# First attention in one hand-written order of TensorE and VectorE, with the Fourier folds inside it

## The chip, the cores and the metric

The kernel runs on one core of a Trainium2 chip, in float32 throughout. Its metric is the device time of one execution in microseconds. Six executions of the kernel before took 844.06 to 846.88 us, with a median of 845.41 us.

## The reference

Two blocks follow each other. The first is a sparse attention over 4 batches, 8 heads, 768 positions and a head dimension of 64. Each query sees the keys less than 16 positions away, and beside them 24 summaries of the whole sequence: for each block of 32 positions the element-wise maximum of its keys and the mean of its values.

```python
k_sum = k.reshape(B, H, nb, block, D).max(axis=3)      # block = 32
v_sum = v.reshape(B, H, nb, block, D).mean(axis=3)
scores_l = where(abs(pos[:, None] - pos[None, :]) < 16, scale * q @ k.T, -1e9)
scores_s = scale * q @ k_sum.T + log(block)
a = softmax(concatenate([scores_l, scores_s]))
x = a @ concatenate([v, v_sum])                        # heads side by side: (4, 768, 512)
```

The second block mixes x by the real part of a Fourier transform over both the sequence and the model dimension, adds it, normalizes, and runs a dense network with 2048 hidden channels. Its weights come in as 64-bit floats.

```python
u = x + real(fft(fft(x, axis=1), axis=2))
un = (u - mean(u)) / sqrt(var(u) + 1e-6)
out = u + maximum(un @ w_ch1, 0) @ w_ch2
```

## The kernel before

The program goes batch by batch: attention of a batch, its Fourier stage, its hidden layer in two halves of eight column groups, and its output products. The stages of different batches overlap. Attention of batch b+1 is issued beside the hidden layer of batch b, and the Fourier stage of b+1 beside the last output products of b. Only the first attention (batch 0) has nothing beside it. It works on four pairs of heads, in a form called wide: 64 queries against 96 positions of keys and 32 rows for the block summaries, so that one product with 128 rows does both.

For each pair, `load` (L568) fetches keys and queries. `prepare` turns them by products with the identity (`qk`, L672), ScalarE copies them out of PSUM into `kt` and `qt`, and VectorE takes the block maxima `km` (L683). `wide_scores` makes the scores in two halves on TensorE (`sc`, L699 and L703), ScalarE takes the exponentials (`p`, L705), and VectorE multiplies with a mask (`p<-p,wide`). `sum_values` brings the block sums of the values into place (`vs` on TensorE, L714; the copy into `vw` on ScalarE, L715). `wide_values` makes the products with the values (`av`, L723), and VectorE divides into `x` (reciprocal at L728, then a multiplication). The block sums of the values come from `block_sums`: four transfers, and additions on GpSimd (POOL), except for one half batch (batch 1, its second), which VectorE adds.

VectorE's `tensor_tensor` is recorded at L560 for all its uses, and GpSimd's at L563, because both go through a helper; transfers through `fetch` are at L547.

The Fourier stage begins with folds on VectorE: sums and differences of the two halves of the sequence (`fold<-x`), then of the two halves of the model dimension, then of mirrored columns (L560, L1006). For batch 0 four products that go nowhere (`busy`, L961; eight rows of the profile) are issued between the folds. Products with the cosine and sine tables follow (`y`, L1024 and L1028), copies into `big` by ScalarE, products over the model dimension (`mx`, L1048, L1050), statistics on VectorE (`bst`, L1056), and normalized, turned columns `u` for the hidden layer (`hx`, `hy`, `hz`, L1111).

While batch 0 passes these stages, `gen_weights` converts the 64-bit weights (loaded as pieces called `words`) on VectorE and ScalarE (L864 to L871) and stores the results for later batches. It starts once the folds of batch 0 are issued.

What sets the order. TensorE's instructions of the first attention stand in program order (`manual_schedule`); other engines' orders are found by a planner, with the Fourier stage ahead by a given priority. The transfers of SP's queue stay in program order up to the hidden layer of batch 0. At most eight transfers are in flight, since SP waits for the one eight places earlier before it issues the next. Buffers set when a load may start: four for keys and queries, two for `vw`.

Of the kernel before, what the change touches and what calls it, by code (L numbers as in the profile page):

```python
# [9 lines left out]
FP = mybir.dt.float32  # L10
# [6 lines left out]
P = 128  # L17
BLOCK = 32
W = 16
# [468 lines left out]
def _main_program(ctx, tc, q, k, v, moe_w_ch1, moe_w_ch2, out):  # L488
# [35 lines left out]

    wide = bpool.tile([P, NC, 2, S], FP, tag="h", name="wide").rearrange("p j h s -> p (j h s)")
    wide, count = wide[:, 0:QB], wide[:, QB:QB + NQ]
# [41 lines left out]
    def load(b, g):  # L568

        qn, kn = (apool.tile([P, 2, NST // 2, 2 * D], FP, tag="nat", bufs=4, name=f"{n}n_{b}_{g}") for n in "qk")  # L570
        for dst, src in ((kn, k), (qn, q)):
            fetch(out=dst.rearrange("p e j n -> p (e j) n"),
                              in_=src[b, 2 * g:2 * g + 2].rearrange("e (j p s) d -> p (e j) (s d)", p=P, s=2))
        nat[b, g] = qn, kn
# [7 lines left out]
    done_weights, sums = [], {}  # L582

    def block_sums(b, gg, g=None):

        rows, heads = (4 * nb, slice(4 * gg, 4 * gg + 4)) if g is None else (2 * nb, slice(2 * g, 2 * g + 2))
        f = BLOCK // 4
        n = f * D
        if done_weights or g == 1:
            raw = room(f"vb_{b}_{gg}") if done_weights else words[:, 4 * n:8 * n]  # L590
            raw = [raw[0:rows, n * i:n * (i + 1)] for i in range(4)]
        else:

            raw = [bpool.tile([P, NC, P], FP, tag="s", bufs=5, name=f"vb_{b}_{gg}_{g}_{i}").rearrange("p n t -> p (n t)")
                   [0:rows] for i in range(4)]
        for i in range(4):
            fetch(out=raw[i], in_=v[b, heads].rearrange("h (n f) d -> (h n) (f d)", f=BLOCK)
                  [:, n * i:n * (i + 1)])
        vb = spool.tile([rows, D], FP, tag="vbs", bufs=2, name=f"vbs_{b}_{gg}_{g}")

        add = tt if (b, gg) == (1, 1) else gtt
# [3 lines left out]
        if (b, gg) == (1, 1):  # L605
# [6 lines left out]
        for n in (2 * gg, 2 * gg + 1) if g is None else (g,):  # L612
            sums[b, n] = vb, sel[0:rows, 0 if g is not None else n % 2]
# [8 lines left out]
    def load_values(b, g):  # L622
        if g % 2 and following(b, g, 1) and (b, g) not in ((0, 1), (1, 1)):
            block_sums(*divmod((b * NP + g + 1) // 2, NP // 2))
        (load_wide_values if is_wide(b) else load_narrow_values)(b, g)

    def load_wide_values(b, g):

        vw = wide_vw(g)
        for e in range(2):  # L630
            off = v[b, 2 * g + e].offset
            parts = [(W, WK, 0, 1), (0, WK, 1, NQ - 1), (0, WK - W, NQ - 1, NQ)]
            for r0, r1, i0, i1 in parts:
                fetch(out=vw[r0:r1, e, i0:i1, 0:D],
                                  in_=bass.AP(v.tensor, off + (QB * i0 - W + r0) * D,
                                              [[D, r1 - r0], [QB * D, i1 - i0], [1, D]]))
# [21 lines left out]
    def prepare(b, g, between=None):  # L658
        qn, kn = nat[b, g]
        kt, km = kt_bufs[g % 2], km_bufs[g % 2]  # L660
        qt = apool.tile([P, S], FP, tag="qt", name=f"qt_{b}_{g}")
        for src, dst in ((kn, kt[:, W:W + S]), (qn, qt)):
            if src is qn and between:
                between()
            if is_wide(b):
                for j0, j1 in ((0, 2), (2, 3)):
                    n = 2 * P * (j1 - j0)
                    ps = abank([P, n], f"qk_{b}_{g}_{j0}")
# [20 lines left out]
    def wide_scores(b, g):  # L689
# [3 lines left out]
        for half in range(2):  # L693
# [10 lines left out]
            for e in range(2):  # L704
                nc.scalar.activation(out=p[:, e, n0:n1], in_=ps[e], func=AF.Exp, scale=SC)  # L705
                tt(p[:, e, n0:n1], p[:, e, n0:n1], wide[:, None, :].to_broadcast([P, NQ // 2, QB]), ALU.mult)
        return p

    def sum_values(b, g):

        ps = abank([P, 2, D], f"vs_{b}_{g}")
        for e in range(2):
            vb, pick = sums[b, g]
            nc.tensor.matmul(ps[WK:P, e], pick[:, D * e:D * e + 32], vb, start=True, stop=True)  # L714
        nc.scalar.copy(out=wide_vw(g)[WK:P, :, :, 0:D],  # L715
                       in_=ps[WK:P, :, None, :].to_broadcast([P - WK, 2, NQ, D]))

    def wide_values(b, g, p, x):
        vw = wide_vw(g)
        av = [abank([P, NST, D1], f"av_{b}_{g}_{e}") for e in range(2)]  # L720
        for n in range(NQ):
            for e in range(2):
                ins = nc.tensor.matmul(av[e][QB * (n % 2):QB * (n % 2 + 1), n // 2, :], p[:, e, n, :], vw[:, e, n, :],  # L723
                                       start=True, stop=True)
        marks["last av"] = ins.ins
        for e in range(2):
            rc = rec[:, b * NP + g, e]
            marks["av", b, g] = nc.vector.reciprocal(out=rc, in_=av[e][:, :, D]).ins  # L728
# [64 lines left out]

    def gen_attention(b):
        x = bpool.tile([P, NST, DM], FP, tag="x", bufs=2, name=f"x_{b}")
        x_of[b] = x
        for g in range(NP):
            p = (wide_scores if is_wide(b) else scores)(b, g)
            yield
            if not is_wide(b):  # L800
                sum_scores(b, g, p[1])
            elif g:
                sum_values(b, g)
            n1, n2 = following(b, g, 1), following(b, g, 2)
            early = (b, g) == (0, NP - 1)
            if early:
                wide_values(b, g, p, x)
            if n1:
                with tc.issue_after(marks["last av"]) if early else ExitStack():
                    prepare(*n1, (lambda: sum_values(0, 0)) if (b, g) == (0, 0) else None)  # L810

            for n in {(0, 1): (), (0, 2): (2,), (0, 3): (2, 3)}.get((b, g), (3,)):
                n = following(b, g, n)
                if n:
                    load(*n)
            yield
            if not early:
                if is_wide(b):
                    wide_values(b, g, p, x)
                else:  # L820
                    values(b, g, *p, x)
            if (b, g) == (0, 0):
                block_sums(0, 1)
                load_raw(2)
# [515 lines left out]
```

## Time and profile before

| What | Time |
|---|---|
| the profiled execution | 845.48 us |
| its span | 843.3 us |
| TensorE busy, matmul | 811.1 us (96%) |
| VectorE busy | 490.8 us (58%) |
| ScalarE busy | 233.0 us (28%) |
| GpSimd busy | 49.8 us (6%) |
| granted TensorE clock, mean | 0.992 |

The span is the time from the first to the last recorded instruction; the execution's own time has some 2.2 us around it. Busy shares are means over stages with different limits. A row of the timeline gives start, length, engine, line, operation, output and inputs, and in brackets the idle time before it with what ended it. The chain of waits follows the work that ended last back to its start. TensorE's f32 products appear as two matmul rows each.

### The profile page before, as it was taken

What the parts mean: (1) busy time and instruction counts of PE and PEld (TensorE: products, weight loads), DVE (VectorE), ACT (ScalarE), POOL (GpSimd) and SP (SyncE); (2) the same over time, 40 slices, a digit from 0 to 9 for tenths busy, and PEclk for the clock granted to TensorE, in tenths of its full rate; (3) what the DMA queues carried; (4) which work ended last, traced back from release to release, by engine and by line L of the source; (5) the groups of instructions that cost most, each with busy time, mean ns of one, the idle gap of its engine ahead of it and who ended that gap; (6) DMA issues with size and microseconds to landing.
All of it is one profiled execution on the core that took longest, in us unless ns stands there. A gap on an engine that the chain in (4) does not pass through costs nothing.

```text
span 843.3 us, 14730 instructions
## 1 busy us (share of the span) xinstructions
PE 811.1 (96%) x6082; PEld 580.7 (69%) x6082; DVE 490.8 (58%) x1117; ACT 233.0 (28%) x497; POOL 49.8 (6%) x57
## 2 busy tenths in 40 slices
PE   7979898999999999999999999999999999999997
PEld 4747555544568865787667875688657885786586
DVE  2478998988898843542447943443338953532352
ACT  2524856452531113122232103220322012101100
POOL 4420002003000200001000000000000000000000
PEclk9999999999999999999999999999999999999999
DMA  7995698988653265453734236403411326205001
GB/s 170 244 275 95 147 311 200 258 258 234 220 182 131 88 203 200 124 110 141 186 101 106 69 125 225 108 25 74 178 57 64 110 61 251 88 1 218 1 26 54
DMA packets 102347, 120.54 MB, mean 143 GB/s; under 512 B 50720, under 2 KB 83712, under 8 KB 102272
## 3 DMA queue, kind: packets, MB, share of 16 engines
q1 hardware_dynamic: 101584, 119.32, 48.1%
q8 instruction: 50, 0.82, 0.4%
q10 hardware_dynamic: 688, 0.20, 0.1%
q14 instruction: 25, 0.20, 0.1%
HBM read 96.96 MB, written 22.54 MB: 142 GB/s over the span
## 4 chain that ended last, share of the span: by engine, by line
PE 81%; DVE 9%; ACT 5%; DMA 2%; issue 1%; ACTq 0%; SPq 0%; DVEq 0%
PE hx L1111 18%; PE ox L1175 16%; PE hz L1111 9%; PE oz L1175 8%; PE hy L1111 4%; PE oy L1175 4%; PE y L1024 4%; PE o L1152 3%; PE sc L740 2%; DVE x L560 2%; PE mx L972 2%; DVE w L560 2%; ACT qt L682 1%; ACT kt L682 1%; PE unt L1089 1%; PE ss L756 1%
## 5 line engine op out<-in xcount | busy, mean ns | idle before, releaser
L1111 PE MATMUL hx<-u,w 128*128 128x384 f32 x512 | 186.3, 492 | 9.6 <-DVE h L560 4.6
L1111 PEld LDWEIGHTS hx<-u,w 128*128 128x128 f32 x512 | 94.2, 190 | 75.2 <-DVE h L560 8.0
L1111 PE MATMUL hz<-u,w 128*128 128x384 f32 x256 | 93.5, 487 | 0.0
L1175 PE MATMUL ox<-w,s 128*128 128x256 f32 x336 | 80.7, 381 | 0.3
L1175 PE MATMUL oz<-w,s 128*128 128x256 f32 x336 | 80.5, 379 | 0.0
L1175 PE MATMUL ox<-w,h 128*128 128x256 f32 x336 | 78.0, 380 | 0.0
L1111 PEld LDWEIGHTS hz<-u,w 128*128 128x128 f32 x256 | 48.4, 190 | 34.8 <-ACT h L1128 1.1
L560 DVE TENSOR_TENSOR x<-ox,x 128x256 f32<-128x256 f32 x84 | 35.3, 423 | 61.2 <-PE ox L1175 61.0
L1175 PEld LDWEIGHTS ox<-w,h 128*128 128x128 f32 x336 | 63.4, 190 | 9.7
L1175 PEld LDWEIGHTS ox<-w,s 128*128 128x128 f32 x336 | 62.7, 190 | 9.5 <-DVE x L560 1.2
L1175 PEld LDWEIGHTS oz<-w,s 128*128 128x128 f32 x336 | 63.5, 190 | 8.4
L560 DVE TENSOR_TENSOR h<-hx,h 128x384 f32<-128x384 f32 x32 | 17.8, 556 | 66.5 <-PE hx L1111 66.5
L560 DVE TENSOR_TENSOR h<-hy,h 128x384 f32<-128x384 f32 x32 | 17.8, 557 | 62.9 <-PE hy L1111 59.7
L1121 ACT COPY h<-hx 128x384 f32<-128x384 f32 x32 | 15.3, 477 | 116.3 <-PE hx L1111 104.6
L1111 PE MATMUL hy<-u,w 128*128 128x384 f32 x128 | 46.5, 486 | 0.0
L1152 PE MATMUL o<-w,h 128*128 128x512 f32 x96 | 43.6, 610 | 0.9 <-DVE w L560 0.9
L1175 PE MATMUL oy<-w,h 128*128 128x256 f32 x168 | 39.7, 379 | 0.0
L1024 PE MATMUL y<-fs,fold 128*128 128x193 f32 x192 | 37.4, 335 | 0.2 <-PE oz L1175 0.2
L1137 ACT ACTIVATE h<-hx 128x384 f32<-128x384 f32 x32 | 15.7, 490 | 79.4 <-PE hx L1111 79.3
L1024 PEld LDWEIGHTS y<-fs,fold 128*128 128x128 f32 x192 | 31.3, 190 | 8.0 <-issue 6.2
L683 DVE TENSOR_REDUCE km<-kt 128x24 f32<-128x768 f32 x16 | 15.2, 952 | 35.3 <-ACT kt L682 24.5
L1111 PEld LDWEIGHTS hy<-u,w 128*128 128x128 f32 x128 | 24.2, 190 | 16.7
(138 smaller groups left out, 1114.3 us busy)
## 6 DMA issues: line engine op xcount, KB each, us to landing
w<-dw SPq DMA_DIRECT2D x44, 896.0 KB, 5.8
words<-in_moe_w_ch_dram SPq DMA_DIRECT2D x32, 512.0 KB, 6.6
dw<-w SPq DMA_DIRECT2D x12, 896.0 KB, 8.4
vw<-in_v_dram SPq DMA_DIRECT2D x47, 192.0 KB, 5.3
kn<-in_k_dram SPq DMA_DIRECT2D x16, 384.0 KB, 4.7
qn<-in_q_dram SPq DMA_DIRECT2D x16, 384.0 KB, 5.6
out_dram<-x SPq DMA_DIRECT2D x24, 256.0 KB, 2.3
fs<-c_fs SPq DMA_DIRECT2D x8, 579.0 KB, 3.8
```

Of the source, the lines that this page charges most:

```text
L560: nc.vector.tensor_tensor(out=out, in0=in0, in1=in1, op=op)
L682: nc.scalar.copy(out=dst[D * e:D * (e + 1), s:S:2], in_=ps[D * s:D * (s + 1)])
L683: nc.vector.tensor_reduce(out=km[:, 0:nb], in_=kt[:, W:W + S].rearrange("p (n f) -> p n f", f=BLOCK), op=ALU.max, axis=AX.X)
L740: nc.tensor.matmul(ps[h][r:r + 64, i, :], kt[rows, o:o + 64], qt[rows, o:o + BLOCK], start=True, stop=True)
L756: nc.tensor.matmul(ps[r:r + 32, :], km[rows, :], qt[rows, S2 * h:S2 * (h + 1)], start=True, stop=True)
L972: nc.tensor.matmul(out, y[:, g], table, start=True, stop=last, skip_group_check=True)
L1024: nc.tensor.matmul(y, fgs[par][:, st, P * g:P * (g + 1)], fs[par][:, g % 2, st, :], start=(st == 0), stop=(st == HT - 1))
L1111: nc.tensor.matmul(ps, w[:, a, kk, :], u[:, r, kk, :], start=start and kk == 0, stop=stop and kk == 1, skip_group_check=True)
L1121: nc.scalar.copy(out=c11, in_=X)
L1137: nc.scalar.activation(out=c21, in_=X, func=AF.Relu)
L1152: nc.tensor.matmul(ps, h[:, n, hf, P * t:P * (t + 1)], wt[2, b, j][:, 2 * hf:2 * hf + 2, :], start=(n, hf) == (0, 0), stop=(n, hf) == (NC ...
L1175: nc.tensor.matmul(ps, left[a][:, n, :], wt[2, b, j][:, r, :], start=start and n == 0, stop=stop and n == NC - 1, skip_group_check=True)
```

## The change

The first attention gets a function of its own, `first_attention`, whose instructions stand in program order on TensorE and on VectorE. A pair's scores are issued before the products with the values of the pair before it. Each pair's columns of `x` are folded over the sequence as soon as they are there (`fold_sequence`), in a place beside the mask; halves are folded when two pairs are there (`fold_halves`), and the mirrored columns after the last pair (`fold_ends`). The products called `busy` are gone.

The block sums of batch 0 are one transfer and five additions on VectorE for each half batch (`add_blocks`), between the two halves of a pair's scores. The block sums of batches 1 and 2 that ran on GpSimd are VectorE additions too, with a reduction at the end (`add = gtt if done_weights else tt`); those of batch 3 stay on GpSimd. For pairs 0 and 3 the copy of the block sums into `vw` is VectorE's.

The loads stand in another order: keys of pair 1 third, tables (`fs`, `fd`, `near`), two weight pieces and the first keys and queries of batch 1 ahead of the values of pair 3. The values' six transfers have the two large ones first. The first pair of batch 1 is prepared in a step of its own after the first attention. The wide transposes take PSUM from the other pool. For batches 1 to 3 the mean and variance come from two ScalarE passes with accumulators in place of VectorE's statistics instructions.

```diff
+    def add_blocks(gg):
+        raw, vb = to_add[gg]
+        n = BLOCK * D // 2
+        while n > D:
+            tt(raw[:, 0:n], raw[:, 0:n], raw[:, n:2 * n], ADD)
+            n //= 2
+        tt(vb, raw[:, 0:D], raw[:, D:2 * D], ADD)
...
+        if b == 0:
+            raw = words[0:rows, 4 * n * gg:4 * n * (gg + 1)]
+            fetch(out=raw, in_=src)
+            to_add[gg] = raw, vb
+            return
...
-        add = tt if (b, gg) == (1, 1) else gtt
+        add = gtt if done_weights else tt
...
-        if (b, gg) == (1, 1):
+        if not done_weights:
             nc.vector.tensor_reduce(out=vb, in_=raw[0].rearrange("p (f d) -> p d f", d=D), op=ADD, axis=AX.X)
...
-                    ps = abank([P, n], f"qk_{b}_{g}_{j0}")
+                    ps = bank([P, n], f"qk_{b}_{g}_{j0}")
...
+            if half == 0 and between:
+                between()
...
-        nc.scalar.copy(out=wide_vw(g)[WK:P, :, :, 0:D],
-                       in_=ps[WK:P, :, None, :].to_broadcast([P - WK, 2, NQ, D]))
+        (nc.vector.tensor_copy if g in (0, NP - 1) else nc.scalar.copy)(
+            out=wide_vw(g)[WK:P, :, :, 0:D], in_=ps[WK:P, :, None, :].to_broadcast([P - WK, 2, NQ, D]))
...
+    def first_attention():
+        x = x_of[0] = bpool.tile([P, NST, DM], FP, tag="x", bufs=2, name="x_0")
+        fold = bpool.tile([P, 7, 2, S2], FP, tag="u", name="fold_0").rearrange("p a k n -> p (a k n)")
+        wt["fold"] = fold[:, 0:3 * HT * DM].rearrange("p (i t d) -> p i t d", i=3, t=HT)
+        p = {0: wide_scores(0, 0, lambda: add_blocks(0))}
+        prepare(0, 1)
+        sum_values(0, 0)
+        load(0, 3)
+        for g in range(NP - 1):
+            p[g + 1] = wide_scores(0, g + 1, (lambda: add_blocks(1)) if g == 1 else None)
+            wide_values(0, g, p[g], x)
+            load_values(*following(0, g, 2))
+            for par in range(2):
+                fold_sequence(par, g)
+            if g == 0:
+                get_tables(0)
+            if g < NP - 2:
+                prepare(0, g + 2)
+                load(1, g)
+                sum_values(0, g + 1)
+            if g == 0:
+                load_raw(2)
+                fetch(out=near, in_=dr["near"].ap().rearrange("p (h i) c -> p h i c", h=2))
+            if g == NP - 3:
+                sum_values(0, g + 2)
+        fold_halves(0, 0)
+        wide_values(0, NP - 1, p[NP - 1], x)
+        for par in range(2):
+            fold_sequence(par, NP - 1)
+            if par:
+                fold_halves(par, 0)
+            fold_halves(par, 1)
+            fold_ends(0, par, wt["fold"][:, par], wt["fold"][:, 2 - 2 * par])
+
+    def fold_sequence(par, g):
+        x, c = x_of[0], slice(P * g, P * (g + 1))
+        tt(early[par][:, :, c], x[:, 0:HT, c], x[:, HT:NST, c], SUB if par else ADD)
+
+    def fold_halves(par, g):
+        sd, zw = early[par], wt["fold"][:, par]
+        lo, hi = slice(P * g, P * (g + 1)), slice(HD + P * g, HD + P * (g + 1))
+        tt(zw[:, :, lo], sd[:, :, lo], sd[:, :, hi], ADD)
+        tt(zw[:, :, hi], sd[:, :, lo], sd[:, :, hi], SUB)
...
-            keep_busy(b, par, sd)
...
-                bst = spool.tile([P, 6], FP, tag="bst", name=f"bst_{b}_{t}")
-                nc.vector.bn_stats(out=bst, in_=x[:, t, :])
-                nc.vector.bn_aggr(out=stat[:, i], in_=bst)
+                nc.scalar.activation(out=un[:, t, :], in_=x[:, t, :], func=AF.Copy, scale=-1.0 / DM,
+                                     accum_out=minus[:, i:i + 1])
+                nc.scalar.activation(out=un[:, t, :], in_=x[:, t, :], func=AF.Square, bias=minus[:, i:i + 1],
+                                     accum_out=var[:, i:i + 1])
...
     load(0, 0)
+    load(0, 1, 1)
+    block_sums(0, 0)
+    load(0, 1, 0)
...
-    with tc.manual_schedule(engines={mybir.EngineType.PE}):
-        drive((first(attn, 6), 1, 0))
...
-    with tc.manual_schedule(engines={mybir.EngineType.PE}):
-        drive((attn, 1, 600), (first(weights, 18), 3, 0))
-    attn = gen_attention(1)
-    drive((gen_fourier(0), 4, 600), (first(weights, 66), 12, 0), (first(attn, 5), 1, 0))
+    with tc.manual_schedule(engines={mybir.EngineType.PE, mybir.EngineType.DVE}):
+        first_attention()
...
+    block_sums(1, 0)
+    def second_attention():
+        prepare(1, 0)
+        load(1, 2)
+        load_values(1, 1)
+        yield
+        yield from gen_attention(1)
+    attn = second_attention()
+    drive((gen_fourier(0), 4, 600), (first(weights, 66), 12, 0), (first(attn, 6), 1, 0))
```

## The prediction

> **What bounds the kernel now.** I read the page first, then busy time by stretch, then the chain of waits over the first 66 us, then the timeline where a wait stood out.
>
> ```profile
> span 843.3 us, 14730 instructions
> PE 811.1 (96%) x6082; PEld 580.7 (69%) x6082; DVE 490.8 (58%) x1117; ACT 233.0 (28%) x497; POOL 49.8 (6%) x57
> ```
>
> TensorE has 32.2 us of idle time in all. The stretches (length, then busy us of PE, PEld, DVE, ACT, POOL, the granted clock, the DMA share, GB/s) say where:
>
> ```profile
> 0.00:10.00 10.00, 8.33 (x66) 5.55 (x68) 1.96 (x14) 3.10 (x5) 2.67 (x9) 1.00 0.77 167
> 10.00:20.00 10.00, 5.82 (x72) 4.07 (x68) 3.03 (x4) 2.33 (x5) 4.80 (x6) 0.89 0.73 177
> 40.00:50.00 10.00, 8.31 (x162) 6.57 (x163) 6.06 (x11) 5.37 (x10) 5.92 (x7) 1.00 1.08 296
> 50.00:60.00 10.00, 6.86 (x47) 3.92 (x43) 8.34 (x12) 0.52 (x4) 0.14 (x1) 0.83 1.15 278
> 80.00:100.00 20.00, 17.46 (x377) 13.70 (x377) 18.50 (x58) 13.19 (x25) 0.00 (x0) 1.00 0.56 115
> 100.00:120.00 20.00, 18.50 (x239) 11.46 (x237) 19.79 (x42) 12.35 (x24) 0.00 (x0) 1.00 0.87 271
> ```
>
> In the first attention (to 51 us) TensorE is idle 8 us and VectorE mostly free, but the DMA engines are at their limit from 20 us on. From 60 to 200 us VectorE is nearly full (Fourier, then the weights' conversion): there it sets the pace with TensorE. After 240 us TensorE stands still for only a few us. The chain (start, length, what) names the early holes:
>
> ```profile
> 10.17 7.20 DMA kn<-in_k_dram
> 17.50 2.57 PE qk L672 x24
> 47.29 0.50 ACT p L705
> 47.80 1.43 ACT vw L715
> 49.26 0.50 ACT p L705
> ```
>
> Pair 1's keys are asked for at 10.17 and land at 17.37; TensorE had ended pair 0's scores at 13.3. The timeline gives the end of the attention, the folds, and three rows for prices used below:
>
> ```profile
> 45.84 0.43 SPq L547 DMA_DIRECT2D near<-c_near  x1
> 46.71 0.38 SPq L547 DMA_DIRECT2D kn<-in_k_dram  x1
> ...
> 49.29 2.03 PE L723 MATMUL av<-vw,p 128*64 128x65 f32 x48 [1.69 <-ACT vw L715]
> 52.56 1.76 DVE L560 TENSOR_TENSOR fold<-x 128x1536 f32<-128x1536 f32 x1
> 54.37 4.54 PE L961 MATMUL busy<-fold,ident 128*128 128x512 f32 x6 [3.06 <-DVE fold L560]
> 64.78 0.55 DVE L1006 TENSOR_TENSOR fold<-fold 128x381 f32<-128x381 f32 x1
> ```
>
> The last attention product ends at 51.3, VectorE folds until 65.3, and only then does it turn to the weights.
>
> **The change, step by step.**
>
> 1. *Loads at the start.* Pair 1's keys are issued third, at about 2 us, and the block-sum values of a half batch in one transfer (2 transfers where there were 12). The 4.2 us wait for keys goes; so does the slow stretch behind it, where 24 transposes took 2.57 us against 1.53 at 27.9: 1.0 us.
>
> 2. *First attention at TensorE's own pace.* By the rows, a pair is 1.53+1.56 transposes, 0.41 sums, 3.9 scores, 1.65 products: 9.1 us. From 13.3: three times 7.4, plus four times 1.65, gives 42.2. VectorE's order is now fixed by hand, and block sums (1024, 512, 256, 128, 64 elements; from 0.68 for 512 and 0.96 for 768, about 2.8 us) stand between two halves of a pair's exponentials' masking. Behind them wait the masking, and behind that the products; also pairs 0 and 3 copy their sums on VectorE (1536 elements, 1.76 by the fold row). VectorE's load for a pair is then about 8 us against 9.1, so most is covered; if it is not, a pair slips by up to 2.8. I add 1.3: **43.5** is TensorE's bound for the end.
>
> 3. *The transfers, the new bound.* SP's queue is in order, and pair 3's values, which waited for their buffer alone, now stand behind the tables (2 fs, fd, near), batch 1's first keys and queries and two weight pieces. Behind them in the queue wait batch 1's next keys, values and weight pieces, which nobody needs before the folds end. Ahead of and with them: 10 keys/queries of 384 KB, 2 sums of 768, 4 values of 560, 1158+768+384 of tables, 1024 of weights, 200 of constants: 11.2 thousand KB, 11.4 MB. Adding the 2 us stretches of the trace, before had moved 11.4 MB at 50.7 us, with about 3 us lost between 16 and 22 us (46 to 180 GB/s). At 290 GB/s throughout it would be 42. By kinds: values at 150 GB/s (6 to 12 us), 512-byte rows at 270 (12 to 14), wide rows at 380 (48 to 54) make 15.3+14.6+13, plus 2.3 to start: 45.2. I take 46.3 for the landing, near the third figure because this queue has fewer small transfers than before. With 1.65 of products and 0.35 of slow clock the attention ends at **48.3**, not 51.25: **-2.95**. Ends: 43.5 (-7.75); and, if the values land only with what stands ahead of them in the queue, 57, where keys issued at 46.71 land now (10.5 us later): 58.9 (+7.6).
>
> 4. *Folds.* From the last product to the last fold VectorE took 14.1 us (51.25 to 65.33). Now only the last pair's share is left: 1.29 for reciprocals and x, 2 sums, 6 halves, 8 ends at 0.50 each (128x384 pitch: two in 1.02), km 0.9, and 0.8 of latency and waiting for the copied keys: 11.0. **-3.1**. The 13 us of other pieces (two block sums 5.6, two copies 3.5, eight fold pieces 4) lie in the first attention, where VectorE was busy 3 to 6 us in 10.
>
> 5. *Batch 1's first pair between.* Its transposes, scores and block scores are now ahead of the Fourier products on TensorE, so those wait for ScalarE's eight copies (4.2 us) and km: about 6.2 us after the last product, where before it was 6.6. No gain there; but km (0.95) no longer comes after the folds, and the 1.20 us that VectorE waited at 69.4 for ScalarE, full of those copies, goes: **-2.15**. The 8 busy products filled a stall and cost nothing.
>
> 6. *Block sums of batches 1 and 2 on VectorE.* Three sets move from POOL: three adds at 0.68 and a reduction of 1.02, 3.07 each. The first, formerly at 43.6 to 49.7 beside the attention, now stands in the full stretch: **+3.07**. The others replace POOL work in that stretch (columns as above):
>
> ```profile
> 126.18 1.27 POOL L563 TENSOR_TENSOR vb_None<-vb_None,vb_None 96x512 f32<-96x512 f32 x1 [74.66 <-DMA vb_None<-in_v_dram]
> 126.30 1.71 DVE L869 SCALAR_TENSOR_TENSOR words<-words 128x512 int32<-128x512 int32 x1 [1.89 <-ACT words L866]
> 130.28 1.50 DVE L864 TENSOR_SCALAR words<-words 128x512 int32<-128x512 int32 x1
> ```
>
> Those take 0.69 and 0.42 elsewhere. Over 126 to 134 VectorE lost 3.0 us, over 191 to 201 2.8. So 6.14 against 5.8: **+0.3** (ends: 0, and 6.1 if none of the slowing mattered).
>
> 7. *Statistics on ScalarE* in batches 1 to 3: 18 times 0.69+0.17 leaves VectorE, 36 passes of about 0.6 (128x512 copy) join ScalarE, at 2 to 6 us in 20 there. TensorE's idle time in those stages is 0.5, 0.1 and 0.1 us. I take 0; ends -0.8 and +3 (one longer tail per batch, if the products beside it run out). The other pool for transposes, and the moved memsets: 0, as those banks stand free.
>
> Sum: -2.95-3.1-2.15+3.07+0.3 = **-4.8**; against the profiled execution (845.48 for a span of 843.3, 0.07 above the median) **840.7**.
>
> *A rule that speaks against it.* The slow clock after the 4.2 us wait (0.50 at 18 to 20 us) cost 1.5 us over transposes and sums; a 3.1 us wait at 132 cost none (clock 1.00 throughout). The Trainium skill, "TensorE: Matmul & The Clock Gate", section "Why this matters for your kernels", wants no idle gap of over about 3 us between bursts, or the clock falls to half. The change drops the products that kept TensorE busy and leaves two such gaps, before the last products and before the Fourier products. Its section "What's actually happening" has full clock come back after about 3.4 us of work. By these both gaps are followed by 3.4 us at half rate, an estimate from that page of 3.4 us lost, and the sum would be 843.8. By the rows I took 0.35 for the first and nothing for the second, which VectorE's folds cover.
>
> **Rivals.** *Slower: the last values come late.* The one queue delivers pair 3's values after 50.1 us. For: the DMA share is already 1.05 to 1.15 from 30 us on. Against: wide rows ran at 355 to 410 GB/s from 46 to 52. Each us late is a us; break-even is an end of attention at 53.1, and landing at 57 gives 851.3. *TensorE's bound holds*, transfers arrive in time: 43.5, thus 835.9. For: fewer transfers; against: step 3's third figure. *The gain is not carried*: VectorE's relief from POOL is not on the path (+5.8), or the weight pieces' transfers (share 1.13 at 120 to 140) set the stage: 846.5 at worst. *The statistics cost*: 843.7, inside the range.
>
> **How the numbers follow.** Forecast 0.50 (838 to 843.5, all faster); TensorE's bound 0.13; not carried 0.17 (0.02 faster, 0.13 same, 0.02 slower); late values 0.20 (0.02 same, 0.18 slower). About 0.2%, 1.7 us, can be told from no change. So faster 0.65, same 0.15, slower 0.20. Range: 835.5, TensorE's bound, to 847, which leaves out most of the late-values case.
>
> **What would show it.** Right: pair 1's transposes follow scores at about 13.3 without a wait; no row for busy products; attention ends at 46 to 50, the wait before it naming values; last fold near 59; first hidden product 5 us before its present 97.6; no POOL rows at 126 or 191 and no VectorE row of 1.5 us beside them. Wrong: values for pair 3 landing after 50, VectorE's block sums ahead of masking holding TensorE in each pair, or the same first hidden product and a longer weights stage.

## The result and the profile after

| | before | after |
|---|---|---|
| median of the runs | 846.19 us | 842.81 us (840.22 to 848.12) |
| the profiled execution, its span | 845.48, 843.3 us | 843.82, 842.0 us |
| ratio to before | | 0.9958, 95% interval 0.9946 to 0.9970 |

The kernel became faster by 3.5 us (2.5 to 4.6); 4.8 were forecast. Below, every kernel is compared by its ratio to the kernel before as timed in its own session, and 0.001 is 0.85 us. The quotient of two medians can differ from that ratio by up to 0.002. The two profiled spans differ by only 1.3 us: single executions scatter by more than most of the steps here are worth, so a row of one execution shows what happened there, and only the ratios say what a kernel gains.

The page of the kernel after, busy time of each engine:

```profile
span 842.0 us, 14695 instructions
PE 811.0 (96%) x6074; PEld 580.0 (69%) x6074; DVE 488.3 (58%) x1117; ACT 255.7 (30%) x567; POOL 12.8 (2%) x21
```

TensorE is as busy as before; GpSimd's 49.8 us have shrunk to 12.8, ScalarE has 23 us more. The timeline of after around the end of the first attention and the folds (start, length, engine, line, operation, in brackets the idle time before and what ended it):

```profile
39.86 1.67 PE L740 MATMUL av<-vw,p 128*64 128x65 f32 x48
51.28 3.07 PE L740 MATMUL av<-vw,p 128*64 128x65 f32 x48 [9.75 <-DMA vw<-in_v_dram]
54.28 1.41 PE L694 MATMUL qk<-ident,kn 128*128 128x128 f32 x6
58.42 0.30 PE L756 MATMUL sc<-qt,kt 64*64 64x32 f32 x4 [1.51 <-ACT qt L696]
61.14 2.94 PE L1070 MATMUL y<-fs,fold 128*128 128x193 f32 x8
...
64.80 0.55 DVE L871 TENSOR_TENSOR fold<-fold 128x381 f32<-128x381 f32 x1
70.00 0.69 DVE L932 SCALAR_TENSOR_TENSOR words<-words 128x512 int32<-128x512 int32 x1 [3.31 <-ACT words L929]
```

TensorE finished three of the four pairs at 41.5 and then stood still for 9.75 us for pair 3's values. The attention ends at 54.35, not at 48.3 as forecast and not at 51.25 as before. The last fold ends at 65.35, where it ended before. The wait also brought the slow clock, as stretches of 2 us show (length, busy us of PE, PEld, DVE, ACT, POOL, granted clock, DMA share, GB/s):

```profile
16.00:18.00 2.00, 1.89 (x34) 1.49 (x32) 1.97 (x4) 0.61 (x2) 0.00 (x0) 1.00 0.41 105
32.00:34.00 2.00, 2.00 (x42) 2.00 (x38) 1.93 (x7) 0.95 (x3) 0.00 (x0) 1.00 0.20 43
44.00:46.00 2.00, 0.00 (x0) 0.00 (x0) 1.04 (x3) 0.20 (x1) 0.00 (x0) 0.80 1.10 362
46.00:48.00 2.00, 0.00 (x0) 0.00 (x0) 0.00 (x0) 0.00 (x0) 0.00 (x0) 0.50 1.25 235
48.00:50.00 2.00, 0.00 (x0) 0.00 (x0) 0.00 (x0) 0.00 (x0) 0.00 (x0) 0.50 1.09 132
52.00:54.00 2.00, 2.00 (x41) 2.00 (x38) 0.00 (x0) 0.00 (x0) 0.00 (x0) 0.50 1.21 307
58.00:60.00 2.00, 1.58 (x10) 0.40 (x12) 2.00 (x6) 1.66 (x5) 0.00 (x0) 0.71 1.03 252
60.00:62.00 2.00, 2.00 (x40) 1.94 (x40) 2.00 (x6) 0.00 (x0) 0.00 (x0) 0.50 1.09 338
64.00:66.00 2.00, 2.00 (x8) 0.72 (x8) 2.00 (x6) 0.19 (x1) 0.00 (x0) 0.58 1.16 249
```

The clock is at half in two places: in the wait and over the last value products (3.07 us against 1.67 for the pair before), and again over the first Fourier products. The first two rows show the transfers slow and then nearly standing still, long before the wait; they are slow once more just before the values land (132 GB/s from 48 to 50 us).

So the change lost its race at the start. Where did it win? The same view in four stretches, of before and then of after:

```profile
0.00:60.00 60.00, 48.82 (x641) 35.36 (x642) 28.65 (x58) 21.60 (x41) 24.19 (x33) 0.94 0.96 232
60.00:100.00 40.00, 37.19 (x480) 28.76 (x479) 34.44 (x88) 23.94 (x56) 0.00 (x0) 1.00 0.63 123
100.00:240.00 140.00, 132.71 (x880) 72.77 (x879) 122.32 (x247) 73.70 (x139) 14.55 (x12) 0.99 0.84 246
```

```profile
0.00:60.00 60.00, 45.41 (x650) 33.84 (x652) 34.51 (x77) 22.64 (x46) 1.47 (x9) 0.91 1.01 226
60.00:100.00 40.00, 37.96 (x459) 29.43 (x458) 34.56 (x96) 19.22 (x46) 0.00 (x0) 0.93 0.66 136
100.00:240.00 140.00, 136.90 (x898) 75.14 (x895) 124.66 (x261) 75.42 (x143) 0.00 (x0) 0.99 0.85 250
```

TensorE's idle time went from 11.2 to 14.6 us in the first 60, and from 7.3 to 3.1 us between 100 and 240, where the first hidden layer runs beside the weights' conversion. In milestones (after minus before): end of attention +3.1 us, last fold 0, first mixing product +3.4, first hidden product +0.6, first output product behind the hidden layer (`ox`) 239.6 against 242.5, -2.9; the last one, at the very end, 834.1 against 836.2, -2.1; the span -1.3. In these two executions the whole gain arises between 98 and 240 us, not where the forecast put most of it, and part of it is lost again behind.

### The profile page after: what moved, and what is told of

It is laid out like the page before. It is cut to its first block, busy times and chain, and to the rows that moved or that the text cites. A ratio compares the mean times of both kernels' runs of the same rounds, so it can differ in the third digit from the quotient of the medians.

```text
span 842.0 us, 14695 instructions
## 1 busy us (share of the span) xinstructions
PE 811.0 (96%) x6074; PEld 580.0 (69%) x6074; DVE 488.3 (58%) x1117; ACT 255.7 (30%) x567; POOL 12.8 (2%) x21
## 4 chain that ended last, share of the span: by engine, by line
PE 86%; ACT 5%; DVE 5%; DMA 1%; SPq 1%; issue 1%; POOL 0%; ACTq 0%; POOLq 0%
PE hx L1171 18%; PE ox L1235 17%; PE hz L1171 9%; PE oz L1235 9%; PE o L1212 5%; PE y L1070 4%; PE hy L1171 4%; PE oy L1235 4%; PE sc L756 2%; PE mx L1027 2%; ACT qt L696 2%; ACT kt L696 2%; PE ss L772 1%; PE y L1074 1%; PE unt L1149 1%; PE av L789 1%
## 5 line engine op out<-in xcount | busy, mean ns | idle before, releaser
L1235 PEld LDWEIGHTS oy<-w,h 128*128 128x128 f32 x168 | 31.9, 190 | 4.3
```

The costliest lines, as they stand in the source:

```text
L1235: nc.tensor.matmul(ps, left[a][:, n, :], wt[2, b, j][:, r, :], start=start and n == 0, stop=stop and n == NC - 1, skip_group_check=True)
```

## The experiments

Three questions: what the late values cost, why the hidden layer's stage got shorter, and whether ScalarE's statistics matter.

**1. Values first.** The tables, two weight pieces and batch 1's first keys and queries are fetched behind pair 3's values.

```diff
-            if g == 0:
+            if g == 1:
                 get_tables(0)
+                load(1, 0)
+                load_raw(2)
+                fetch(out=near, in_=dr["near"].ap().rearrange("p (h i) c -> p h i c", h=2))
...
-                load(1, g)
+                if g:
+                    load(1, g)
...
-            if g == 0:
-                load_raw(2)
-                fetch(out=near, in_=dr["near"].ap().rearrange("p (h i) c -> p h i c", h=2))
```

> The changed kernel with one thing moved: the tables, two weight pieces, the near mask and batch 1's first keys and queries are fetched after the values of pair 3, not ahead of them. Queue theory (the 9.75 us wait of the last products is only the place of the values in SP's queue): the wait before the last products falls below 1.5 us, the attention ends at 43 to 45 instead of 54.4, the last fold at 54 to 57 instead of 65.4, and the whole is 4 to 9 us below the changed kernel (about 834 to 839). Rival, transfers bound the stretch whatever their order: the tables then arrive late, the Fourier products start at 58 to 61 as now, and the whole stays within 1.5 us of the changed kernel.

Measured: 843.61 us, ratio 0.9976 (0.9958 to 0.9995); no gain over after's 0.9958, where 4 to 9 us were expected. Yet the queue theory was right up to the folds: the wait is gone, the last two pairs' products run as one row at full speed (`38.93`, 3.07 us for 96), and the attention ends at 42.0, 12.3 us earlier than in after. The first hidden product is 7.7 us earlier, the last of the hidden layer 5.6 us (232.8 against 238.4). Then TensorE stops. Stretches of this kernel, and its chain of waits (start, length, what):

```profile
220.00:240.00 20.00, 15.76 (x53) 9.96 (x52) 19.93 (x38) 9.58 (x20) 0.00 (x0) 0.94 0.75 288
240.00:260.00 20.00, 20.00 (x111) 15.59 (x110) 13.51 (x32) 6.90 (x26) 0.00 (x0) 0.89 0.27 93
```

```profile
218.93 1.00 DVE w L562 x3
...
223.97 0.48 DVE h L562
...
234.27 1.76 DVE fold L562
236.29 2.29 DVE fold L562 x3
238.83 3.01 PE y L1071 x8
```

Unbroken VectorE work from 212 to 224, and then batch 1's folds: VectorE is full (19.93 of 20), TensorE waits 3.32 us for the folds and pays for it with a slow clock. It ends the weights at 233, after at 236.6, though the attention ended 12 us earlier. In after the same 20 us show TensorE at 19.98. Up to 240 us TensorE stands still for 21.9 us in this kernel and for 19.7 in after: 8.7 instead of 14.6 in the first 60, but 13.1 instead of 5.1 from there on. So the early time was lost again, and by these rows to VectorE. That theory is tested in 5 and 6.

**2. Sums back on GpSimd** (the first set of batch 1 and both of batch 2).

```diff
-        add = gtt if done_weights else tt
+        add = tt if (b, gg) == (1, 1) else gtt
...
-        if not done_weights:
+        if (b, gg) == (1, 1):
```

> The changed kernel with the block sums of batch 1's first half and of batch 2 back on GpSimd. Theory A (what the change won, it won in the weights' stage, since GpSimd's additions slowed VectorE and TensorE waited for it): slower than the changed kernel by 2 to 4 us, VectorE rows of 1.5 us beside GpSimd's rows again. Theory B, the prediction's price (the sums cost VectorE 9.2 us and the slowing only 5.8): faster than the changed kernel by 2 to 3.5 us.

Measured: 845.33, ratio 0.9982 (0.9962 to 1.0002): some 2 us of after's gain are lost, at the low end of theory A and just clear of nothing (0.0024, give or take 0.0023 by the two intervals); theory B is excluded. TensorE's idle time from 100 to 240 rises from 3.1 to 5.2 us. GpSimd's adds again slow VectorE's rows beside them (timeline of this kernel):

```profile
190.60 1.28 POOL L565 TENSOR_TENSOR vb<-vb,vb 96x512 f32<-96x512 f32 x1 [57.59 <-DMA vb<-in_v_dram]
190.85 1.58 DVE L934 SCALAR_TENSOR_TENSOR words<-words 128x512 f32<-128x512 uint32 x1
```

**3. Statistics on VectorE** in batches 1 to 3, as before the change.

```diff
-                nc.scalar.activation(out=un[:, t, :], in_=x[:, t, :], func=AF.Copy, scale=-1.0 / DM,
-                                     accum_out=minus[:, i:i + 1])
-                nc.scalar.activation(out=un[:, t, :], in_=x[:, t, :], func=AF.Square, bias=minus[:, i:i + 1],
-                                     accum_out=var[:, i:i + 1])
+                nc.vector.bn_stats(out=bst, in_=x[:, t, :])
+                nc.vector.bn_aggr(out=both[:, i], in_=bst)
```

> The changed kernel with VectorE's statistics instructions back in batches 1 to 3. The prediction's price: within 0.8 us of the changed kernel. Rival, the two ScalarE passes relieve VectorE where TensorE waits: slower by 1 to 3 us. Other rival, they lengthen the tail: faster by 1 to 3 us.

Measured: 841.5, ratio 0.9947 (0.9929 to 0.9964). No difference from after that these runs can tell: the statistics are beside TensorE's work, as costed.

**4. The kernel before with its sums on VectorE**, all three sets, and then **with batch 2's two sets only**.

```diff
-        add = tt if (b, gg) == (1, 1) else gtt
+        on_vector = b > 0 and not done_weights
+        add = tt if on_vector else gtt
...
-        if (b, gg) == (1, 1):
+        if on_vector:
```

> The kernel before with one part of the change alone: the block sums of batch 1's first half and of batch 2 on VectorE. Theory A: faster than before by 2 to 4 us, with TensorE's idle time between 120 and 140 us, now 3.1, below 1.5. Theory B: slower by 0 to 3 us.

```diff
-        add = tt if (b, gg) == (1, 1) else gtt
+        on_vector = (b, gg) == (1, 1) or (b == 2 and not done_weights)
+        add = tt if on_vector else gtt
```

> The kernel before, with one part of the change alone: the two block sums of batch 2 are added on VectorE, the first one of batch 1 stays on GpSimd inside the first attention. Theory S, these two sums are most of the whole change's gain: with all three sets moved TensorE's idle time from 100 to 240 us fell from 7.3 to 4.7 us and 2.2 us were lost in the first attention; without that loss the time is 2 to 3 us below before, 843.5 to 844. The prediction's step 6, 6.14 us of own work against 5.8 us of slowing: within 0.7 us of before.

Measured: 846.01, ratio 0.9998 (0.9983 to 1.0014), with all three; 845.41, ratio 0.9981 (0.9967 to 0.9996), with two. The stretch from 100 to 240 us, of the first and then of the second:

```profile
100.00:240.00 140.00, 135.30 (x954) 73.86 (x947) 123.78 (x256) 76.02 (x143) 0.00 (x0) 0.99 0.86 253
```

```profile
100.00:240.00 140.00, 135.29 (x895) 73.57 (x893) 123.81 (x258) 75.45 (x142) 0.00 (x0) 0.99 0.85 252
```

TensorE's idle time there falls from 7.3 to 4.7 us in both; from 120 to 140 us it is 2.6 in the first, where less than 1.5 was expected. The first kernel gains nothing, where 2 to 4 us were expected. Its attention ends at 53.6 and its first hidden product is at 100.8 instead of 97.5. In the second, whose first set stays on GpSimd, the two are at 52.1 and 99.5, also later than before. So about 1.3 of the 3.3 us in these rows go with the set that stands in the old first attention, which fits the 1.4 us between the ratios. By its ratio moving the two sets of batch 2 alone gives -1.6 us (-0.3 to -2.8); the gain of 2 to 3 us that the expectation named is at the edge of that, and step 6's zero just outside.

**5. Less work for VectorE: the mask step left out**, in after and in the kernel with values first.

```diff
-        nc.vector.tensor_scalar(out=man, in0=high, scalar1=0x000FFFFF, scalar2=None, op0=ALU.bitwise_and)
...
-        nc.scalar.activation(out=tmp[:, 1, :], in_=man, func=AF.Copy, bias=1.0, scale=2.0 ** -20)
+        nc.scalar.activation(out=tmp[:, 1, :], in_=high, func=AF.Copy, bias=1.0, scale=2.0 ** -20)
```

> The changed kernel without the step that masks the mantissa bits of the weights' high words: ScalarE reads the unmasked words, so the first batch's weights, and with them the output, are not the reference's. VectorE loses 32 steps of 0.42 us (0.34 apart), 11 to 13 us, between 65 and 237 us; nothing else is taken away. Theory V, VectorE sets the pace of the weights' stage and of the first folds behind it: TensorE's idle time from 100 to 240 us falls from 3.1 us to under 1.5, and the time falls by 2 to 3 us, to 840 to 841. Theory T, TensorE itself sets the pace there: within 1 us of the changed kernel's 842.8.

> The same step left out of the kernel that fetches pair 3's values first (there the attention ended 12 us earlier, but the time stayed at 843.6, with VectorE ending the weights at 231 us and TensorE waiting for its folds at 238.8). Again the first batch's weights and the output are not the reference's. Theory V: VectorE's 11 to 13 us less let the early gain through; the last weight step is at 222 or earlier, the 3.3 us wait for the folds goes, and the time is at least 4 us below 843.6, near 837. Rival, the early gain is lost to something else (transfers, TensorE's own order of work): 841 to 844, and the last hidden product again at about 228.

**6. A shorter conversion**, again in both.

```diff
-        nc.vector.tensor_scalar(out=ex, in0=high, scalar1=0x7FF00000, scalar2=None, op0=ALU.bitwise_and)
-        nc.vector.tensor_scalar(out=man, in0=high, scalar1=0x000FFFFF, scalar2=None, op0=ALU.bitwise_and)
-        nc.scalar.activation(out=ex, in_=ex, func=AF.Relu, bias=rebias, scale=8.0)
-        nc.scalar.activation(out=tmp[:, 1, :], in_=man, func=AF.Copy, bias=1.0, scale=2.0 ** -20)
...
-        tt(dst, tmp[:, 1, :], tmp[:, 0, :], ALU.mult)
+        nc.vector.tensor_scalar(out=tmp[:, 0], in0=high, scalar1=0x07FFFFFF, scalar2=3, op0=ALU.bitwise_and,
+                                op1=ALU.logical_shift_left)
+        nc.vector.scalar_tensor_tensor(out=tmp[:, 1], in0=high, scalar=-(1 << 31), in1=tmp[:, 0],
+                                       op0=ALU.bitwise_and, op1=ALU.bitwise_or)
+        nc.vector.scalar_tensor_tensor(out=dst.bitcast(I32), in0=low, scalar=29, in1=tmp[:, 1],
+                                       op0=ALU.logical_shift_right, op1=ALU.bitwise_or)
```

> Pair 3's values first, and the conversion of the weights shortened: three steps on VectorE (0.42, 0.69, 0.69 us) that shift and join the bits of the 64-bit words, where there were five (2.91 us in all) and two on ScalarE. It truncates instead of rounding and holds for weights below 2 in size, as the reference's are; the time is that of the whole computation. Theory V, VectorE held back the early attention's gain: it loses 32 times 1.11, 35 us, the last weight step comes before 215 us, the wait for the first folds at 238 goes, and the time falls below the 838.25 of the run without the mask, to 831 to 837. Rival, TensorE or the transfers of the weights are the next bound and were reached already without the mask: 837.5 to 839.5.

> The changed kernel with the short conversion alone (three steps on VectorE for five, none on ScalarE; truncates, for weights below 2 in size). Its TensorE stood still for 3.1 us between 100 and 240 and 2.0 between 60 and 100, and leaving the mask out gave nothing (842.7). Theory: TensorE sets the pace there and the late start stays, so 839.5 to 842.8. Rival, VectorE still sets the pace: 836 to 839, as low as the same step with the values first.

Measured (median, ratio to before, interval):

| VectorE's conversion | values late, as in after | values first |
|---|---|---|
| as it is | 842.81, 0.9958 (0.9946 to 0.9970) | 843.61, 0.9976 (0.9958 to 0.9995) |
| without the mask | 842.69, 0.9942 (0.9921 to 0.9962) | 838.25, 0.9904 (0.9885 to 0.9923) |
| short | 838.64, 0.9935 (0.9910 to 0.9961) | 833.79, 0.9871 (0.9850 to 0.9892) |

Read across: with the conversion as it is, values first gain nothing (+1.5 us by the ratios); without the mask 3.2 us; with the short one 5.4 us. Read down: with late values the lighter conversion is worth 1.4 and 2 us, both within the intervals; with values first 6.1 and 8.9 us. The early attention and the lighter conversion give 7.4 us together, more than the two alone add up to. That is what two engines that take turns as the bound look like. The mask is VectorE's alone, and leaving it out lets 3.2 us of the early time through: so VectorE's work held back a good part of the 12 us. The short conversion also takes two steps from ScalarE, so its 5.4 us are not shown to be VectorE's alone.

The times came out as theory T has it for late values without the mask, and as theory V has it with values first; the rows fit less well. Values first without the mask end the weights at 230.9 us, where 222 was expected, and still wait 1.58 us for the folds. With the short conversion the wait for the folds is gone and the weights end at 225.5, where 215 was expected. Late values without the mask leave TensorE 4.2 us of idle time from 100 to 240, where theory V wanted less than 1.5. Late values with the short conversion don't decide: the median, 838.64, is in the rival's range (836 to 839), and the ratio, 840.7 beside the 846.19 of before, in the theory's.

With values first and the short conversion, TensorE's idle time from 100 to 240 us is 2.4 us, and the chain names a weight piece as the next wait:

```profile
217.58 5.99 DMA words<-in_moe_w_ch_dram
223.60 0.44 DVE words L927
224.06 0.70 DVE words L930
```

Values first with the short conversion is the best kernel here: 833.79 us, 1.29% (1.08 to 1.50) below before. It truncates the weights (relative error up to 1.2e-7) and holds only for weights below 2 in size; a kernel for any weights would need a test for that.

**7. Products in the wait.** Unread products on TensorE ahead of pair 3's value products, to keep the clock up: 20 of them, then 10.

```diff
         fold_halves(0, 0)
+        ps = bank([P, DM], "busy")
+        for i in range(20):
+            nc.tensor.matmul(ps, ident, p[NP - 2][:, 0, 0:8, :].rearrange("p n c -> p (n c)"), start=True, stop=True)
         wide_values(0, NP - 1, p[NP - 1], x)
```

> The changed kernel with 20 products of 512 columns, whose result nobody reads, on TensorE ahead of pair 3's value products: 8.6 us at 0.43 us each, into the wait of 9.75 us. Clock theory: the granted clock stays at 1.00 through the wait, the last 48 value products take 1.65 us instead of 3.07, and the attention ends 1.4 us earlier, at 53 with the values landing at 51; last fold near 64, first hidden product near 97. If that is carried, the time is 1 to 2 us below 842.8. Rival, the early time is not on the path: clock and product times as above, and the time within 0.7 us of 842.8. If the values land well before the 20 products end, the attention ends no earlier.

> The changed kernel with 10 instead of 20 unread products ahead of pair 3's value products; one of them took 0.87 us in the run with 20, so 8.7 us into the wait of 9.75. Clock theory: clock 1.00 through the wait, the last value products 1.67 us instead of 3.07, the attention ends near 52.9 instead of 54.35, with the values landing at 51. For the whole: theory C (the clock's loss is on the path and carried to the end) 841 to 841.8; rival (what is early there is taken back by VectorE in the weights' stage, as the 12 us of the values-first run were) within 0.8 us of 842.8.

Twenty took twice the time that was expected (each is two rows of 0.43 us) and held up the value products themselves. The timelines, with twenty and with ten:

```profile
41.05 17.43 PE L839 MATMUL busy<-p,ident 128*128 128x512 f32 x40
58.41 1.67 PE L740 MATMUL av<-vw,p 128*64 128x65 f32 x48
```

```profile
40.68 8.85 PE L839 MATMUL busy<-p,ident 128*128 128x512 f32 x20
50.34 1.80 PE L740 MATMUL av<-vw,p 128*64 128x65 f32 x48 [0.81 <-DMA vw<-in_v_dram]
```

The clock stayed at 1.00 through the wait in both, and the value products took 1.67 and 1.80 us instead of 3.07. With twenty the attention ends at 60.1 and the time is 852.0, ratio 1.0062 (1.0042 to 1.0083): being 5.7 us later than after costs 8.8. With ten the attention ends at 52.1, 2.2 us earlier than in after, and the ratio is 0.9957 (0.9939 to 0.9974), the same as after's. The median, 841.66, lies between what the two theories gave; by the ratio the earlier end is not carried, and an effect of up to 1.7 us can't be excluded. The profiled execution, the third shortest of this kernel's twelve, does carry it: first hidden product 95.0 instead of 98.2, span 838.1 instead of 842.0. So this stays open.

**8. The first set of batch 1 alone back on GpSimd.**

```diff
-        add = gtt if done_weights else tt
+        on_vector = not done_weights and (b, gg) != (1, 0)
+        add = tt if on_vector else gtt
```

> The changed kernel with only the first block sum of batch 1 back on GpSimd (there it stood at 66.6 to 73.9 us, 7 us of GpSimd); batch 2's two stay on VectorE. Prediction's step 6, its four rows of 3.07 us on VectorE at 73.8 to 77.1 are on the path: first hidden product about 3 us earlier than 98.15 and the time 3 us lower, a ratio near 0.992. Rival, covered: VectorE waited 0.73 us for the mixing products just after those rows, so TensorE was later than VectorE there; ratio within 0.001 of the changed kernel's 0.9958. With both this set and batch 2's on GpSimd the ratio was 0.9982, so the rival also has batch 2's two sets alone worth about 2 us.

Measured: 843.76, ratio 0.9974 (0.9957 to 0.9991). Neither theory's number: 1.4 us slower than after by the ratios, with 0 not excluded, and step 6's gain of 3 us excluded. The first hidden product does come 2 us earlier (96.1), but in this execution the attention already ended 1.6 us earlier (52.8), since the values landed earlier, so that 0.5 us are left for the set. The stage behind it is longer (`ox` 144.4 us after it, against 141.5 in after), and TensorE's idle time from 100 to 240 is 5.6 us instead of 3.1. Why a set that ends at 72 us shows there was not settled; one profiled execution may also be off by a microsecond. With experiment 2, batch 2's two sets would be worth 0.7 us in after by difference, not the 2 us that the rival had, though the intervals leave room for both.

## Why the prediction was right, and where it was not

The time of 842.81 lies within the likeliest case (838 to 843.5), but that is in part luck: step 3 came out about 6 us worse than priced and step 6 about 5 us better, and step 5's gain is not seen.

*Step 1, loads at the start, right.* Pair 1's transposes follow pair 0's scores at 13.30, the clock is 1.00 from 10 to 20 us, and TensorE is busy 9.62 us there instead of 5.82.

*Step 2, TensorE's own pace, right.* Three pairs were done at 41.5; with values in time (values first) the attention ended at 42.0, where 43.5 was the bound. The block sums between the halves took 2.9 us (2.8 forecast) and cost TensorE no wait of more than 0.5 us.

*Step 3, the transfers, failed.* The queue had to move 11.4 MB, and adding the 2 us stretches it had moved 11.55 MB when the values landed at 51.1. The bytes were right; the rate was not. The step assumed that the standstill of before (46 to 180 GB/s at 16 to 22) would not come back. It did, in three places: 100 and 105 GB/s from 14 to 18, 115 and 43 from 30 to 34, and 132 and 81 from 48 to 51.1. The values landed 4.8 us behind the forecast of 46.3; their transfers were issued only from 42.34 on, as the chain of waits of after shows (start, length, what):

```profile
35.61 0.87 DVE km L697
36.48 1.57 SPq L549
38.11 3.26 SPq L549
41.42 0.82 SPq L549
42.34 0.38 SPq L549
...
44.63 6.51 DMA vw<-in_v_dram
51.28 3.07 PE av L740 x47
```

By this chain the issue of the first weight piece waited 0.9 us for VectorE's `km`, which stands behind the block sums of the second half batch on VectorE. Then came the issues ahead of the values: 1.57 and 3.26 us for the two weight pieces, then `near`. So -2.95 was +3.1. The 54.35 lies between the ends given, 43.5 and 58.9, but far from the value taken. That their place in the queue made the values late is shown by values first. That kernel also has fewer bytes ahead of them, so it doesn't tell the volume from the queue's own time.

The sum had no term for that time. SP's issue rows fill 92% of the stretch from 5 to 49.5 us in after, and 79% in before. The six transfers of a pair's values took 8.79, 7.15, 7.19 and 7.11 us to issue in after, and 3.06, 5.01, 7.39 and 3.23 in before. For pair 2 after and pair 3 before:

```profile
25.60 7.19 SPq L549 DMA_DIRECT2D vw<-in_v_dram  x6
39.00 3.23 SPq L547 DMA_DIRECT2D vw<-in_v_dram  x6
```

Why the issues became slower was not tried; the two large transfers of a pair now stand first, and one of them alone took 5.08 us.

*The clock rule.* The rows put 0.35 us for the slow clock at the value products; it cost 1.4 (3.07 against 1.67), and the filled waits show that the clock was the reason. The Trainium skill, "TensorE: Matmul & The Clock Gate", section "Why this matters for your kernels", which wants no idle gap of over about 3 us, was the better guide here: 9.75 us of idle time took the clock to 0.50. The section "What's actually happening" has about 3.4 us of work before full clock returns; here the clock was still 0.50 at 52 to 54 and 1.00 in the row of 56 to 58, after products from 51.28 on, which agrees roughly. Over the Fourier products it does not: if the clock changed once within each of the rows of 58 to 60 (0.71) and 64 to 66 (0.58), it was at half for some 6.8 us, an estimate from these rows, with TensorE busy nearly throughout.

*Step 4, folds, right.* From the last product to the last fold 11.0 us were forecast and 11.0 were measured (54.35 to 65.35). Only this made good the lost 3.1 us.

*Step 5, failed in part.* The Fourier products start 6.8 us after the last product (6.2 forecast; in before it was 7.5, at 58.71, not the 6.6 that the prediction read). They run at half clock for over 4 us, and the first mixing product is 3.4 us later than before, about as much as the end of the attention (3.1). Whether the half clock cost anything here is not shown. The 1.20 us that VectorE waited for ScalarE did not go: VectorE waits 3.31 us for ScalarE's conversion step, which stands behind the copies of the late Fourier products. At the first hidden product step 5 and the first set of step 6 were priced at +0.9 together, and +0.6 was measured; the runs don't separate the two there.

*Step 6, block sums, failed in sign.* +3.37 was priced. The two sets of batch 2 give -1.6 us in the kernel before; all three back on GpSimd cost after 2.0 us; the first set's +3.07 is excluded by the last experiment. Two things were missed. The first set stands at 73.8 to 78.2, where VectorE then waits 0.73 us for the mixing products, so some of it had cover; how much is open. And the slowing by GpSimd was counted as 5.8 us of VectorE's time against 6.14 of own work, as if a microsecond of VectorE were worth the same wherever it falls. But in before TensorE waited for VectorE in that stage (3.1 us for `h` in one wait at 132, 1.7 for `vs`, 0.9 for a weight); in after no single wait is over 1 us. So in before something that TensorE needed stood behind VectorE's rows, and the row of the longest such wait comes just after GpSimd's adds:

```profile
135.43 1.56 PE L1111 MATMUL hx<-u,w 128*128 128x384 f32 x4 [3.11 <-DVE h L560]
```

That the planner put the sums on VectorE where nothing was waiting is likely from this, but not shown. The Trainium skill, "Perfetto Trace Analysis", section "Optimizing Scalar/DVE Operations", says that GpSimd and VectorE share a read port, so that moving work between them might not help; the rows of 1.58 us beside GpSimd's adds, against 0.69 elsewhere, agree with a shared port, but here moving the adds did help, by the 1.6 us above.

*Step 7, statistics, right:* 0.

Of the rivals, *late values* came true in its mechanism: the values landed at 51.1, past its 50.1, and the attention ended at 54.35, past the break-even of 53.1. By the prediction's own sum this meant slower than before. The largest part of what made it faster, as far as the runs show, is step 6, about 5 us better than priced: +3.1 (transfers), -3.1 (folds) and -2.0 (sums, give or take 2) make -2.0, of the 3.5 measured. *TensorE's bound* came true in the kernel with values first and shows that its 835.9 was wrong as a time: 843.6. In these runs an attention that ended 5.7 us later cost 8.8 us, and one that ended 12.3 us earlier gained nothing. So *the gain is not carried* came true for values first, but not for the reasons it gave: VectorE's conversion was full there, and its relief from GpSimd was on the path.

What stays open is the other 1.5 us: with all three sums on GpSimd the changed kernel keeps a ratio of 0.9982, at the edge of what the runs can tell, and no run isolates where that comes from. VectorE's waits for ScalarE's conversion step fell from 9.1 us to 4.9, which would fit, but that was not tried by itself.

## What to carry to other kernels

A microsecond saved ahead of a stage may count only if the engine that bounds that stage has less to do, too; test this by taking work from that engine with and without the early start, as in the table under 6. When several engines share a queue of transfers, price the landing of the last needed transfer by the queue's issue rows and waits as well, and not by its bytes alone. An operation moved between two engines that slow each other is to be priced by who waits for the slowed rows, not by the sum of durations.

## What the runs showed of the hardware that was not expected

The clock also fell to half without a single wait of 3 us. In the kernel with ten products in the wait, TensorE ran from 50.34 to 54.3 with breaks of at most 0.3 us, waited 1.52 us for copied queries, and went on; the stretches show the clock:

```profile
52.00:54.00 2.00, 1.70 (x14) 1.19 (x12) 1.83 (x5) 1.26 (x3) 0.14 (x1) 1.00 1.26 275
54.00:56.00 2.00, 0.48 (x7) 0.25 (x5) 1.36 (x3) 1.93 (x5) 0.00 (x0) 1.00 1.40 167
56.00:58.00 2.00, 2.00 (x43) 1.23 (x41) 2.00 (x7) 1.09 (x4) 0.00 (x0) 0.78 1.36 175
58.00:60.00 2.00, 2.00 (x7) 2.00 (x8) 2.00 (x6) 0.00 (x0) 0.00 (x0) 0.50 1.09 286
```

TensorE was busy 0.48 of 2 us there, and the half clock came 2 us later, over products that ran without a break. After shows the same (0.57 of 2 us at 56 to 58, longest wait 1.51 us, clock 0.50 from 60 to 64), there over the Fourier products. Later in after the clock is 0.57 and 0.58 in the rows from 120 to 124, with no wait longer than 0.6 us ahead of them; TensorE was busy 1.42 and 1.41 of 2 us in the rows from 116 to 120. In the kernel before, a single wait of 3.11 us, until 135.4, had left the clock at 1.00 in every row of 2 us from 132 to 138. So the length of the longest wait alone doesn't tell, in these runs, whether the clock falls; what does was not tried.
